# Dummy matmuls of 512 columns, a rectify moved to ScalarE and denominators a slot up, in the start of a cosFormer attention and mixture-of-experts kernel

## Chip, cores, metric

One NeuronCore of one Trainium2 chip. The metric is the device time of one execution in microseconds (us). Names used below: PE is TensorE (PEld its weight loads), DVE is VectorE, ACT is ScalarE, POOL is GpSimd, SP is SyncE.

## The reference

Linear (cosFormer) attention over 8 batches, whose output is the input of a dense mixture of 8 experts with Sinkhorn-balanced gates. Cut to what matters here:

```python
# attention: B, H, S, D = 8, 8, 576, 64
def phi(x, c, s):
    r = np.maximum(x, 0.0)                     # the "rectify"
    return np.concatenate([r * c, r * s], axis=-1)
q_p, k_p = phi(q, cos_w, sin_w), phi(k, cos_w, sin_w)
kv  = np.einsum('bhsf,bhsd->bhfd', k_p, v)
z   = np.sum(k_p, axis=2)
num = np.einsum('bhsf,bhfd->bhsd', q_p, kv)
den = np.einsum('bhsf,bhf->bhs', q_p, z)[..., None] + 1e-06
x   = num / den                                # then (4608, 512)
# gates: exp(x @ w_gate), 8 Sinkhorn rounds -> P
# for e in 8 experts: out += P[:, e] * (relu(x @ w1[e]) @ w2[e])
```

## The kernel before

The kernel is tuned already: PE works nearly all the time. Expert 0's matmuls for each batch (`ffn1`, `ffn2`) are woven in "slots" with the attention of the next batch. The parts that the change and the argument touch are these.

Dummy matmuls on a tile of ones keep PE busy while the first data is prepared (the first 80 run from 1.14 to 7.34 us), and are meant to keep its clock up. It is 1.00 in the trace from 4.4 to 21.5 us:

```python
def keep_busy(n):
    for _ in range(n):
        te.matmul(out=idle_ps[:, 0:P], lhsT=ones_sq[:], rhs=ones_sq[:], start=True, stop=True)
# [...] called with 80 at the start, 3 after each of 12 groups of turns, then 8, 5 and 18
```

k is rectified in place and multiplied by cos and sin. q likewise; the q of the first two batches is transposed by PE ("turns"), that of the later ones by DMA out of a pool of three `q_p` buffers:

```python
def prep_k(b, hk):
    k16 = loaded["k", b, hk]
    if b >= 2:
        se.activation(out=k16, in_=k16, func=AF.Relu)
    else:
        ve.tensor_scalar(out=k16, in0=k16, scalar1=0.0, scalar2=None, op0=ALU.max)

def prep_q(b, hk):
    # [...] (rectify on DVE if b >= 2)
    q_p = qp_pool.tile([P, C, 2, D], F16, name="q_p")          # qp_pool has bufs=3
    ve.tensor_tensor(out=q_p[:], in0=q16..., in1=cs, op=ALU.mult)
    if by_dma:                                                  # b >= 2
        qTs[b, hk] = q_pTs[(b * HK + hk) % len(q_pTs)]
        nc.sync.dma_start(out=qTs[b, hk], in_=q_p[:]..., transpose=True)
```

The inputs are loaded by POOL's queue, as early as buffers allow. The loads of the fourth batch (b = 3) are written at slot (1, 0), and in time run from 33 us on:

```python
            if j == 0:
                for half in range(2):
                    at(1, 0, load, b + 2, half)        # here b is 1: the fourth batch's q, k, v
            elif b + 2 < B:
                for half in range(2):
                    at(j, 11 + half, load, b + 2, half, "qkv", True)
```

`sums` makes k_p.T v, `denominators` multiplies z with qT and prepares the reciprocals `hl`, and `attend(b, hk)` reads `hl` (which makes its matmuls easy to find in the trace) and leaves the batch's part of x. As far as the traces were read, each engine runs its instructions in the written order: in that of the changed kernel a `k_p` of DVE stands behind a `q_p` that waits 1.91 us (shown below).

The softmax here doesn't subtract the row's maximum and nothing guards it: scores larger than these inputs give would overflow.

Of the kernel before, what the change touches and what calls it, by code (L numbers as in the profile page):

```python
# [25 lines left out]
def kernel(  # L26
# [11 lines left out]
    P = nc.NUM_PARTITIONS  # L38
# [12 lines left out]
    TCH = 512  # L51
# [129 lines left out]
    with ExitStack() as p1:  # L181
# [15 lines left out]
        def load(b, half, names="qkv", held_back=False):  # L197
# [24 lines left out]
        ones_sq = cs_pool.tile([P, P], F16, name="ones_sq")  # L222
# [3 lines left out]
            out=ident[:], in_=ones_sq[:], pattern=[[-1, P]], compare_op=ALU.is_equal,  # L226
# [15 lines left out]

        def keep_busy(n):


            for _ in range(n):
                te.matmul(
                    out=idle_ps[:, 0:P], lhsT=ones_sq[:], rhs=ones_sq[:], start=True, stop=True
                )

        idle_ps = ps_y.tile([P, Dm], FP32, name="y_ps")
        keep_busy(80)

        wrap = cs_pool.tile([P, C], FP32, name="wrap")
        ve.tensor_scalar(
            out=wrap[:], in0=gidx[:], scalar1=float(S), scalar2=None, op0=ALU.is_ge
# [3 lines left out]
            out=sval[:], in0=wrap[:], scalar=-float(S), in1=gidx[:],  # L260
# [9 lines left out]
        for hh in range(2):  # L270
            ve.tensor_copy(
                out=cs_half[hh * HP : (hh + 1) * HP, :, :, hh],
# [18 lines left out]
        with nc.allow_low_precision("sums of zeros and ones"):  # L291
            ve.tensor_reduce(
                out=lo[:], in_=rows[:, :, 1, :], axis=AX.XY, op=ALU.add, negate=True
# [3 lines left out]
                out=sel[:], in0=rows[:, 0:3, 0, :], in1=rows[:, 0:3, 1, :], op=ALU.add  # L297
            )
        ve.tensor_copy(
            out=spread.rearrange("p j hk hh d -> p (j hk hh) d"),  # L300
# [32 lines left out]

        def prep_k(b, hk):
            k16 = loaded["k", b, hk]
            if b >= 2:
                se.activation(out=k16, in_=k16, func=AF.Relu)
            else:
                ve.tensor_scalar(out=k16, in0=k16, scalar1=0.0, scalar2=None, op0=ALU.max)
# [27 lines left out]
        def prep_kp(b, hk):  # L367
            k16 = loaded.pop(("k", b, hk))
            k_p = kp_pool.tile([P, C, 2, D], F16, name="k_p")
            ve.tensor_tensor(  # L370
                out=k_p[:], in0=k16.unsqueeze(2).to_broadcast([P, C, 2, D]),
                in1=cs, op=ALU.mult,
            )
            kps[b, hk] = (
                k_p, v_augs[(b * HK + hk) % len(v_augs)] if b else loaded.pop(("v", b, hk))
            )
# [146 lines left out]
        def attend(b, hk):  # L523

            parts = ((0, 2 * C3), (2 * C3, C))
            rb_ps = [ps_s.tile([P, 512], FP32, name="small_ps") for _ in parts]
            rb = rb_pool.tile([P, C * HP], FP32, name="rb")
            for i, (c0, c1) in enumerate(parts):
                for j in range(c0 // C3, c1 // C3):
                    te.matmul(  # L530
                        out=rb_ps[i][:, (j * C3 - c0) * HP : ((j + 1) * C3 - c0) * HP],
                        lhsT=spread[0:96, j, hk].rearrange("p hh d -> p (hh d)"),
                        rhs=hls[b][:],
                        start=True,
                        stop=True,
                    )
                se.copy(out=rb[:, c0 * HP : c1 * HP], in_=rb_ps[i][:, 0 : (c1 - c0) * HP])
            num_ps = [ps_s.tile([P, 512], FP32, name="small_ps") for _ in parts]
            for i, (c0, c1) in enumerate(parts):
                for hh in range(2):  # L540
                    te.matmul(
                        out=num_ps[i][hh * HP : (hh + 1) * HP, 0 : (c1 - c0) * HP],
                        lhsT=kvs[b][0][:, hk, hh, :],
                        rhs=qTs[b, hk][:, c0:c1, hh * HP : (hh + 1) * HP],
                        start=True,
                        stop=True,
                    )
                ve.tensor_tensor(
                    out=xT[:, hk, b * S + c0 * HP : b * S + c1 * HP],
                    in0=num_ps[i][:, 0 : (c1 - c0) * HP],  # L550
                    in1=rb[:, c0 * HP : c1 * HP],
                    op=ALU.mult,
                )
# [25 lines left out]
        def at(block, slot, fn, *args):  # L579
            todo.setdefault((block, slot), []).append((fn, args))  # L580
# [19 lines left out]
        prep_kp(0, 1)  # L600
        denominators(0, range(0, 4))
        keep_busy(8)
        for hk in (2, 3):
            prep_k(0, hk)
# [16 lines left out]
        for hk in range(HK):  # L621
            attend(0, hk)
            for kt in ((), (0,), (1,), (2, 3))[hk]:
                for ft, h_ps in enumerate(first_ps):
                    te.matmul(
                        out=h_ps[:],
                        lhsT=w0[0][:, kt, ft * P : (ft + 1) * P],
                        rhs=xT[:, kt, 0:TCH],
                        start=(kt == 0),
                        stop=(kt == KT - 1),  # L630
                    )
                    if kt == KT - 1:
                        se.activation(out=hT[:, ft, 0:TCH], in_=h_ps[:], func=AF.Relu)
            for i in ((), (), (0,), (1, 2, 3))[hk]:
                prep_k(1, i)
                prep_kp(1, i)
        for hk in range(3):
            prep_q(1, hk)

        for j in range(B):  # L640
            b = j + 1
            if j == 0:

                def sums_first(half):
                    sums_made(1, half, sums_begun(1, half))

                for hk in range(HK):
                    for i in range(3):
                        at(0, (5, 6, 7, 7)[hk], turn, 1, hk, i, i != 1)
                    if hk == 0:  # L650
                        at(0, 5, prep_q, 1, 3)
                    if hk == 1:
                        at(0, 6, prep_v, 1, 0, se.copy)
                        at(0, 6, prep_v, 1, 2, ve.tensor_copy)
                    if hk == 2:
                        at(0, 7, prep_v, 1, 1, se.copy)
                        at(0, 7, prep_v, 1, 3, ve.tensor_copy)
                for half in range(2):
                    at(0, 7, sums_first, half)
                at(0, 9, denominators, 1)  # L660
                at(0, 10, gates, 0)
                for hk in range(HK):
                    at(0, 11 + hk, attend, 1, hk)
            elif b < B:
                if j == 1:
                    for hk in (2, 3):
                        at(j, 0, prep_q, b, hk)
                        at(j, 0, prep_k, b, hk)
                        at(j, hk - 2, prep_kp, b, hk)
                        at(j, hk - 2, prep_v, b, hk, se.copy)  # L670
                    at(j, 1, sums, b, 0)
                    at(j, 3, sums, b, 1)
                else:
                    at(j, 0, sums, b, 1)
                at(j, 5 if j == 1 else 3, denominators, b)
                for hk in range(HK):
                    at(j, (8 if j == 1 else 6) + 2 * hk, attend, b, hk)
            if j:
                at(j, 5, gates, j)
            if j == 0:  # L680
                for half in range(2):
                    at(j, 3, load, b + 1, half)
                for slot, fn, hk, *args in (
                    (12, prep_q, 0), (12, prep_k, 0), (13, prep_q, 1), (13, prep_k, 1),
                    (14, prep_kp, 0), (14, prep_v, 0, se.copy), (15, prep_kp, 1),
                    (15, prep_v, 1, se.copy),
                ):
                    at(j, slot, fn, b + 1, hk, *args)
            elif b + 1 < B:
                for slot, fn, hk in (  # L690
                    (3, prep_k, 0), (4, prep_q, 0), (4, prep_k, 1), (5, prep_q, 1),
                    (7, prep_kv, 0), (7, prep_k, 2), (7, prep_q, 2), (9, prep_q, 3),
                    (9, prep_k, 3), (9, prep_kv, 1), (11, prep_kv, 2), (13, prep_kv, 3),
                ):
                    at(j, slot + (j == 1), fn, b + 1, hk)
                at(j, 15 if j == 1 else 14, sums, b + 1, 0)
            if j == 0:
                for half in range(2):
                    at(1, 0, load, b + 2, half)
# [3 lines that stand above are left out]
# [490 lines left out]
    while stream:  # L1193
        _, pair, name = stream.pop(0)
# [32 lines left out]
```

## Time and profile before

| | before |
|---|---|
| time, median of 3 runs | 987.17 us (986.81 to 987.29) |
| span of the profiled run | 985.7 us |
| PE busy | 968.6 us (98%) |
| stop of PE with no releaser, at 17.5 us | 2.82 us |
| granted clock of 0.5 after it | 21.5 to 24.9 us |

From the page of the kernel before: the line of busy times (us, share of the span, number of instructions), and the shares of the chain that ended last.

```profile
PE 968.6 (98%) x7923; PEld 677.0 (69%) x7923; DVE 805.8 (82%) x1833; ACT 565.3 (57%) x1263; POOL 60.6 (6%) x82
...
PE 94%; DVE 2%; ACT 2%; issue 1%; POOL 0%; DMA 0%; ACTq 0%; SPq 0%; DVEq 0%; POOLq 0%
```

A kernel at 98% on its longest engine has only its start, its few waits and its end to give. The waits are read from the timeline of PE. Its columns are start and duration in us, engine, line, operation, output and inputs, shapes, count; in brackets the idle time of PE just before and what ended it. Of the kernel before:

```profile
16.66 0.79 PE L109 MATMUL y_ps<-ones_sq 128*128 128x128 f16 x11
20.27 0.55 PE L109 MATMUL y_ps<-ones_sq 128*128 128x128 f16 x7 [2.82 <-issue]
20.65 0.41 PE L109 MATMUL small_ps<-hl,acc_hi 96*128 96x192 f16 x3
...
31.95 0.68 PE L109 MATMUL small_ps<-ident,q_p 128*128 128x128 f16 x9 [0.76 <-DVE q_p L109]
...
44.01 0.42 PE L109 MATMUL small_ps<-hl,acc_hi 96*128 96x192 f16 x3 [0.35 <-DVE hl L109]
...
55.42 0.74 PE L109 MATMUL small_ps<-acc_lo,k_p 64*128 64x65 f16 x36
...
57.93 1.06 PE L109 MATMUL small_ps<-q_pT,zsel 128*32 128x192 f16 x24
...
62.02 0.41 PE L109 MATMUL small_ps<-hl,acc_hi 96*128 96x192 f16 x3
```

The stop of 2.82 us falls between the 11th and the 12th of 18 dummies, which wait for nothing. The lines that read `hl` at 20.65, 44.01 and 62.02 us are the first attends of the first, second and third batch: three milestones.

From the windows of the kernel before (window, its length, busy us and instructions of PE, PEld, DVE, ACT and POOL, then the granted TensorE clock, the DMA engines' share, GB/s):

```profile
18.00:20.00 2.00, 0.00 (x0) 0.00 (x0) 0.00 (x0) 0.00 (x0) 0.59 (x1) 1.00 1.28 196
20.00:22.00 2.00, 1.62 (x17) 1.06 (x16) 0.47 (x1) 0.70 (x2) 1.43 (x2) 0.88 1.42 198
22.00:25.00 3.00, 3.00 (x13) 1.19 (x11) 1.18 (x4) 0.70 (x2) 1.43 (x2) 0.51 1.23 208
```

After the stop the clock is at half for 3.41 us. The DMA engines are full all the while (share over 1).

### The profile page before, as it was taken

How to read it: one execution, taken by the hardware profiler on the slowest of the kernel's cores; microseconds unless marked ns; L12 is line 12 of the kernel's file. 1: busy time of each engine (PE TensorE's matmuls, PEld its weight loads, DVE VectorE, ACT ScalarE, POOL GpSimd, SP SyncE). 2: the span in 40 equal slices, each digit the busy share in tenths (PEclk: the TensorE clock that was granted, in tenths of full speed). 3: DMA queues.
4: the chain of work that ended last, by engine and by line, in shares of the span. 5: the costliest groups of instructions: out<-in, count | busy, mean ns of one | idle time of the engine just before them, and what ended most of it. 6: DMA issues, size and time to landing. Idle time of an engine off the chain costs nothing.

```text
span 985.7 us, 20379 instructions
## 1 busy us (share of the span) xinstructions
PE 968.6 (98%) x7923; PEld 677.0 (69%) x7923; DVE 805.8 (82%) x1833; ACT 565.3 (57%) x1263; POOL 60.6 (6%) x82
## 2 busy tenths in 40 slices
PE   8999999989999999999999999999999999999997
PEld 6444444447777777777777777777777777777775
DVE  5786774789889888988789888988888888987886
ACT  4676665467776555555555555555555555555551
POOL 6311110010000000000000000000000000000001
PEclk9999999999999999999999999999999999999999
DMA  9969990741013410133103400223103401104535
GB/s 164 206 120 161 156 152 10 136 76 48 34 41 67 88 29 26 50 67 67 50 25 68 91 25 25 60 60 66 49 25 75 85 25 35 39 25 119 130 88 123
DMA packets 80337, 73.56 MB, mean 75 GB/s; under 512 B 33264, under 2 KB 72176, under 8 KB 80240
## 3 DMA queue, kind: packets, MB, share of 16 engines
q0 software_dynamic: 27232, 30.94, 19.9%
q1 hardware_dynamic: 52768, 41.06, 16.9%
q8 instruction: 62, 1.02, 0.4%
q10 hardware_dynamic: 240, 0.26, 0.1%
q14 instruction: 35, 0.29, 0.1%
HBM read 83.12 MB, written 12.98 MB: 97 GB/s over the span
## 4 chain that ended last, share of the span: by engine, by line
PE 94%; DVE 2%; ACT 2%; issue 1%; POOL 0%; DMA 0%; ACTq 0%; SPq 0%; DVEq 0%; POOLq 0%
PE rows_ps L109 34%; PE h_ps L109 28%; PE copied_ps L109 11%; PE p_ps L109 11%; PE y_ps L109 6%; PE small_ps L109 4%; ACT acc_lo L109 0%; DVE k_p L109 0%; DVE acc_hi L900 0%; POOL hs_last L915 0%; DVE P_tok L109 0%; ACT hT L109 0%; DMA out_dram<-acc_lo 0%; DVE colp L109 0%; ACT u L109 0%
## 5 line engine op out<-in xcount | busy, mean ns | idle before, releaser
L900 DVE SCALAR_TENSOR_TENSOR acc_lo<-rows_ps,P_tok,acc_lo 128x512 f32<-128x512 f32 (+1 forms) x322 | 203.1, 639 | 74.8 <-PE rows_ps L109 74.6
L109 PEld LDWEIGHTS <-H 128*128 128x128 f16 x2080 | 203.0, 98 | 83.1 <-issue 1.2
L836 ACT CAST u<-h_ps 128x384 f16<-128x384 f32 x288 | 137.8, 478 | 131.1 <-PE h_ps L109 131.1
L109 PEld LDWEIGHTS <-w1e 128*128 128x128 f16 x1632 | 156.6, 98 | 67.5 <-issue 7.6
L830 DVE CUSTOM_DVE_ANT_0 H<-p_ps,u 128x384 f16<-128x384 f32 x329 | 180.8, 550 | 6.7 <-PE p_ps L109 6.6
L109 PEld LDWEIGHTS <-hs 128*128 128x128 f16 x1500 | 146.6, 98 | 56.2
L109 PE MATMUL h_ps<-S,w1e 128*128 128x384 f16 x672 | 164.1, 326 | 1.1 <-ACT u L109 0.9
L109 PE MATMUL p_ps<-xT,T 128*128 128x384 f16 x672 | 164.1, 326 | 0.1
L109 PE MATMUL h_ps<-xT,w1e 128*128 128x384 f16 (+1 forms) x616 | 150.5, 351 | 0.8 <-ACT hT L109 0.6
L109 PE MATMUL rows_ps<-V,H 128*128 128x256 f16 x1000 | 150.0, 273 | 0.7 <-DVE acc_hi L900 0.7
L109 PE MATMUL rows_ps<-w2e,hs 128*128 128x256 f16 x1000 | 150.0, 273 | 0.0
L868 ACT ACTIVATE H<-h_ps 128x384 f16<-128x384 f32 x144 | 70.7, 491 | 95.0 <-PE h_ps L109 95.0
L109 PEld LDWEIGHTS <-T 128*128 128x128 f16 x1008 | 98.1, 98 | 29.2 <-issue 2.8
L109 PE MATMUL rows_ps<-w2e,H 128*128 128x256 f16 (+1 forms) x568 | 91.2, 285 | 0.0
L849 ACT COPY copied_ps<-h_ps 128x384 f32<-128x384 f32 x144 | 67.5, 468 | 35.2 <-PE h_ps L109 35.2
L859 ACT ACTIVATE H<-copied_ps 128x384 f16<-128x384 f32 x144 | 70.9, 492 | 20.3 <-PE copied_ps L109 20.3
L109 PE MATMUL h_ps<-S,T 128*128 128x384 f16 x336 | 81.8, 325 | 0.3 <-ACT copied_ps L109 0.3
L109 PE MATMUL copied_ps<-xT,w1e 128*128 128x384 f16 x336 | 82.1, 326 | 0.0
L109 PE MATMUL copied_ps<-w2e,H 128*128 128x256 f16 x504 | 75.5, 272 | 0.0
L109 PE MATMUL rows_ps<-V,hs 128*128 128x256 f16 x500 | 75.0, 272 | 0.0
L900 DVE SCALAR_TENSOR_TENSOR acc_lo<-copied_ps,P_tok,acc_lo 128x256 f32<-128x256 f32 x126 | 60.0, 476 | 0.5
L900 DVE SCALAR_TENSOR_TENSOR acc_hi<-rows_ps,P_tok,acc_hi 128x512 f32<-128x512 f32 (+1 forms) x56 | 41.2, 736 | 20.5 <-PE rows_ps L109 19.7
(147 smaller groups left out, 953.2 us busy)
## 6 DMA issues: line engine op xcount, KB each, us to landing
S<-x_saved SPq DMA_DIRECT2D x108, 192.0 KB, 2.4
out_dram<-acc_lo SPq DMA_DIRECT2D x62, 128.0 KB, 2.4
w1e<-in_moe_w_dram POOLq DMA_DIRECT2D x7, 1024.0 KB, 8.9
w2e<-in_moe_w_dram POOLq DMA_DIRECT2D x7, 1024.0 KB, 9.6
q_ld<-in_q_dram POOLq DMA_DIRECT2D x16, 288.0 KB, 7.5
k_ld<-in_k_dram POOLq DMA_DIRECT2D x16, 288.0 KB, 8.3
v_ld<-in_v_dram POOLq DMA_DIRECT2D x16, 288.0 KB, 9.6
x_saved<-S SPq DMA_DIRECT2D x18, 192.0 KB, 1.9
```

The costliest lines, as they stand in the source:

```text
L109: i = getattr(self.engine, name)(*args, **kwargs)
L830: latest = ve._custom_dve(TENSOR_ADD_SAT, out=out, in0=ps[:, 0:TU], in1=t[:], s0=FP32_MAX, s1=0.0)
L836: se.copy(out=t[:], in_=ps[:, 0:TU])
L849: se.copy(out=Y[:, 0:TU], in_=X[:, 0:TU])
L859: se.activation(out=h11, in_=Y[:, 0:TU], func=AF.Relu)
L868: se.activation(out=h12, in_=X[:, 0:TU], func=AF.Relu)
L900: ve.scalar_tensor_tensor(out=a, in0=rows, scalar=P_tok[:, g, self.e : self.e + 1], in1=a, op0=ALU.mult, op1=ALU.add,)
```

## The change

Its intent: fewer PE instructions for the same dummy time (so that instructions are fetched in time), less work for DVE in front of the second batch's q, and the denominators early enough for DVE's reciprocal chain to be hidden.

```diff
         def keep_busy(n):
-            for _ in range(n):
+            for cols in [TCH] * (n // 4) + [n % 4 * P] * (n % 4 > 0):
                 te.matmul(
-                    out=idle_ps[:, 0:P], lhsT=ones_sq[:], rhs=ones_sq[:], start=True, stop=True
+                    out=idle_ps[:, 0:cols],
+                    lhsT=ones_sq[:],
+                    rhs=ones_sq[:, 0:1].to_broadcast([P, cols]),
+                    start=True,
+                    stop=True,
                 )
@@ prep_k
-            if b >= 2:
+            if b:
                 se.activation(out=k16, in_=k16, func=AF.Relu)
@@ after attend(0, hk) and its share of ffn1
-            for i in ((), (), (0,), (1, 2, 3))[hk]:
+            for i in ((), (0,), (1, 2), (3,))[hk]:
                 prep_k(1, i)
+            for i in ((), (0,), (1,), (2, 3))[hk]:
                 prep_kp(1, i)
@@ slots of the first block
-                at(0, 9, denominators, 1)
+                at(0, 8, denominators, 1)
```

## The prediction

> **What bounds the kernel now.** TensorE is 968.6 of 985.7 us busy (98%, the page); the chain that ended last is 94% PE. From 60 us on, 10 us windows show PE busy throughout, but for about 4 us in the Sinkhorn part. The change touches only the first 60 us: what it saves moves the end one for one, but is a few us.
>
> The timeline of PE shows three losses there:
> 1. PE stops from 17.45 to 20.27 us, 2.82 us, amid the 18 dummies, releaser "issue". I read it as an instruction fetch: the instruction queue moved a packet from 17.78 to 18.72. [...] packets of 16 KiB, 256 PE instructions apart (boundaries at the 189th, 445th, 701st). While loads fill the DMA engines, each starts about 3.7 us after PE crosses a boundary (8.24 to 11.82, 14.07 to 17.78, 20.27 to 23.97) and serves some 2.5 us later: 6.2 us for 256 instructions, which dummies of 56 ns and 64-row matmuls of 16 ns (two instructions each) outrun.
> 2. After that stop the granted clock is 0.5 from 21.5 to 24.9 us; matmuls of 512 columns stand 0.42 us apart instead of 0.22: some 1.4 us.
> 3. DVE's k rectify and k_p hold q_p: PE idles 0.76 us at 31.2; later 0.35 us at 43.7, for hl.
>
> **What changes.** Dummies: the same columns and time, 212 PE instructions fewer. The boundaries shift: the 189th instruction is now in the first key sums (about 11.4 us), the 445th in the second half of the kv sums (16.3 us), the 701st past the turns, where PE is slow. The fetch triggered at 11.4 should serve about 17.5. So the stop does not vanish: I expect 1.2 us (0.5 to 2) there, and the first attend at 18.9 instead of 20.65: 1.7 us. A stop of 1.2 us should not drop the clock (1.1 us idle around 31 us did not): 1.4 us more.
>
> ScalarE takes four k rectifies: DVE loses 4 x 0.30 us, ACT gains 4 x 0.6 us. Three fall among the rb copies and delay the last of these by some 0.3 us. The fourth is queued behind four hT activations; k_p(3) and q_p wait for it: PE's idle before the first turns grows from 0.76 to about 1.5 us. Net cost 0.5 us.
>
> The denominators a slot up put three y_ps blocks (0.9 us each) behind them instead of two; DVE's den chain (2.5 us) is then covered: 0.35 us.
>
> **Sum.** 1.7 + 1.4 - 0.5 + 0.35 = 2.9 us. Predicted 984.3 us, range 982.2 to 986.3. Faster by over 2%: 0.01; within 2%: 0.98; slower: 0.01.
>
> **Right if** the profile shows: the "issue" stop near 16 to 17.5 us, about 1.2 us long; no clock of 0.5 near 21 to 25; the fourth k rectify after hT; PE's idle before the first turns longer, that before the second batch's attend gone; from 60 us on the same events 3 us earlier.
>
> **Wrong if** the fetch comes sooner (no stop: 1.3 us better) or later, or the stop still halves the clock (1.4 us worse); if the fourth rectify costs PE more, or the longer idle at 27 to 29 us halves the clock; if loads, whose landing doesn't move, become the limit; or if a shifted boundary makes a new stop before 45 us.

The "boundaries" are every 256th PE instruction, matmuls and weight loads counted: the pages show 62 packets of 16 KB on the instruction queue q8 for 15846 of them before the change, and 61 for 15634 after it, one per 256.

## More of the kernel before

The lines at 55.42 (sums) and 57.93 (denominators) of the third batch run without a wait.

From the list of DMA issues of the kernel before, 44 to 60 us: the transposes of the third batch's q, their number and the median us from issue to landing.

```profile
q_pT<-q_p SPq DMA_TRANSPOSE x4, 3.5
```

## The result, and the profile after

Ratios are the mean time of one kernel's fast runs over that of the other's fast runs of the same rounds, so they are not quite the ratio of the medians quoted beside them.

| | before | after |
|---|---|---|
| time, median of 4 runs each | 986.99 us (986.72 to 987.29) | 986.49 us (986.31 to 987.08) |
| ratio, 95% interval | | 0.9996 (0.9979 to 1.0013) |
| span of the profiled run | 985.7 us | 985.4 us |
| first attend of batch 1, 2, 3 | 20.65, 44.01, 62.02 us | 19.23, 41.69, 62.63 us |

The forecast was 984.3 us, at most 986.3. The measured 986.49 us lies outside: nearly nothing was gained. The profiled run was the slowest of the four, but the others gained no more than 0.7 us against the median before.

From the page of the changed kernel:

```profile
PE 967.8 (98%) x7817; PEld 671.3 (68%) x7817; DVE 805.8 (82%) x1829; ACT 566.7 (58%) x1267; POOL 60.6 (6%) x82
...
PE 94%; DVE 2%; ACT 2%; DMA 1%; issue 0%; POOL 0%; SPq 0%; ACTq 0%; DVEq 0%; POOLq 0%
```

106 matmuls and as many weight loads fewer, as meant. In the chain that ended last "issue" gave its 1% to "DMA". These shares are rounded, so the line is only a hint: a wait for instructions may have been traded for a wait for transfers. The timeline of PE of the changed kernel, the same places as before:

```profile
16.00 0.88 PE L109 MATMUL small_ps<-v_ld,k_p 64*128 64x64 f16 x48
17.78 0.53 PE L109 MATMUL small_ps<-v_ld,k_p 64*128 64x64 f16 x24 [0.91 <-issue]
...
19.23 0.41 PE L109 MATMUL small_ps<-hl,acc_hi 96*128 96x192 f16 x3
...
30.15 0.68 PE L109 MATMUL small_ps<-ident,q_p 128*128 128x128 f16 x9 [1.61 <-DVE q_p L109]
...
41.69 0.41 PE L109 MATMUL small_ps<-hl,acc_hi 96*128 96x192 f16 x3
...
53.09 0.46 PE L109 MATMUL small_ps<-acc_lo,k_p 64*128 64x65 f16 x18
55.26 0.46 PE L109 MATMUL small_ps<-acc_lo,k_p 64*128 64x65 f16 x18 [1.70 <-DVE k_p L109]
...
57.48 0.68 PE L109 MATMUL small_ps<-q_pT,zsel 128*32 128x192 f16 x18
59.25 0.35 PE L109 MATMUL small_ps<-q_pT,zsel 128*32 128x192 f16 x6 [1.10 <-DMA q_pT<-q_p]
...
62.63 0.41 PE L109 MATMUL small_ps<-hl,acc_hi 96*128 96x192 f16 x3
```

Up to 41.69 us all goes as foreseen, and PE is 2.32 us ahead. Then come two waits that the kernel before does not have, 1.70 and 1.10 us, and at the third milestone PE is 0.61 us behind. From there on the two traces run in step: at PE's last instruction the changed kernel is 0.76 us behind (981.05 against 980.29 us), and only the tail of the last stores differs in its favour. The windows of the changed kernel show the full clock where it was at half:

```profile
20.00:22.00 2.00, 1.75 (x13) 0.94 (x12) 1.64 (x5) 1.58 (x5) 0.79 (x2) 1.00 1.44 204
22.00:25.00 3.00, 3.00 (x23) 1.36 (x21) 2.51 (x6) 2.44 (x6) 1.43 (x2) 1.00 1.22 203
```

What does `k_p` wait for at 53 us? The timeline of DVE of the changed kernel:

```profile
51.56 0.30 DVE L109 TENSOR_SCALAR q_ld<-q_ld 128x576 f16<-128x576 f16 x1
53.77 0.76 DVE L109 TENSOR_TENSOR q_p<-q_ld,acc_hi 128x1152 f16<-128x1152 f16 x1 [1.91 <-DMA q_pT<-q_p]
54.45 0.75 DVE L109 TENSOR_TENSOR k_p<-k_ld,acc_hi 128x1152 f16<-128x1152 f16 x1
```

The fourth `q_p` of the third batch goes into the first of three buffers, and so waits for the transpose that reads it; `k_p`, which PE needs, stands behind it in DVE's order. And the transposes are late. The DMA issues of the changed kernel from 44 to 60 us, and its DMA queues from 46 to 49 us (packets, MB, share of 16 engines):

```profile
q_pT<-q_p SPq DMA_TRANSPOSE x4, 5.4
```

```profile
q0 software_dynamic: 570, 0.62, 121.0%
```

They take 5.4 us at the median instead of 3.5. The first was issued at 46.09 us, and in the 3 us from 46 to 49 not one packet of the transposes' queue (q1) moved: q0, the loads from POOL, had all of the DMA engines. In the trace its packets start at 49.11 us, 3.0 us after the issue; in the kernel before the first was issued at 48.41 us and its packets start at 49.75, 1.3 us after. In both the stream of loads dies down near 49 to 51 us. It does so at the same time because the loads had filled the DMA engines almost since the start (their share is 1.02 or more in every window read from 4 to 49 us, in both kernels); PE's lead did not shorten it: from 49 to 50 us q0 still starts 157 packets before the change and 151 after it, from 50 to 51 us 55 and 61.

The second wait, 1.10 us, is of another kind. The last packet of the loads starts at 52.37 us, before the third and fourth transposes are issued (52.69 and 54.62 us). The DMA queues of the changed kernel from 56 to 59 us:

```profile
q1 hardware_dynamic: 1050, 0.26, 103.5%
q8 instruction: 1, 0.02, 2.4%
```

No load moves here. Beside the transposes there is one packet of 16 KB of q8, the instruction queue whose packets go with PE's count (one per 256 of its instructions, above), from 56.57 to 57.71 us. From 57 us on the transposes' packets stall (20 took over 1 us), and the fourth transpose lands at 59.21 us, 4.6 us after its issue (3.5 us in the kernel before). There PE's wait ends. (A landing is here the last of the transfer's 16 records in the trace.) So the traces point to the loads for the first wait, and beside the second they show an instruction fetch that fell into a transpose. The runs below test the first; none was made to test the second by itself.

### The profile page after: what moved, and what is told of

Read it like the earlier page. It is cut to its first block, busy times and chain, and to the rows that moved or that the text cites. A ratio compares the mean times of both kernels' runs of the same rounds, so it can differ in the third digit from the quotient of the medians.

```text
span 985.4 us, 20168 instructions
## 1 busy us (share of the span) xinstructions
PE 967.8 (98%) x7817; PEld 671.3 (68%) x7817; DVE 805.8 (82%) x1829; ACT 566.7 (58%) x1267; POOL 60.6 (6%) x82
## 4 chain that ended last, share of the span: by engine, by line
PE 94%; DVE 2%; ACT 2%; DMA 1%; issue 0%; POOL 0%; SPq 0%; ACTq 0%; DVEq 0%; POOLq 0%
PE rows_ps L109 34%; PE h_ps L109 27%; PE copied_ps L109 11%; PE p_ps L109 11%; PE y_ps L109 6%; PE small_ps L109 4%; DMA q_pT<-q_p 1%; ACT hT L109 0%; DVE acc_hi L904 0%; POOL hs_last L919 0%; DVE P_tok L109 0%; DMA out_dram<-acc_lo 0%; DVE colp L109 0%; ACT u L109 0%; ACT acc_lo L109 0%
```

## The experiments

**Theory A**: PE's lead is taken back because the third batch's q transposes now come before the end of the stream of loads (whose last are the fourth batch's v) and wait for it. **Theory B**: the rectify on ACT loses the lead, by way of the changed order. Two further questions are whether the stop at 17 us is an instruction fetch, and what the fourth rectify costs. Each kernel ran 5 timed rounds (6 for one) on the same chip as the others of its group; the kernel before on those chips had medians of 987.5, 986.58 and 987.09 us.

The milestones of all profiled runs (first attend of the second and third batch, read from the timeline of PE; then when the third batch's first transpose was issued, and when it landed) tell most of the story:

| kernel | 2nd batch, us | 3rd batch, us | between | transpose issued | landed |
|---|---|---|---|---|---|
| before | 44.01 | 62.02 | 18.01 | 48.41 | 52.55 |
| after | 41.69 | 62.63 | 20.94 | 46.09 | 53.68 |
| dummies_only | 42.06 | 62.28 | 20.22 | 46.47 | 53.05 |
| rectify_only | 43.60 | 61.40 | 17.80 | 48.01 | 52.97 |
| denoms_only | 44.99 | 62.77 | 17.78 | 49.38 | 53.19 |
| moved | 40.21 | 62.30 | 22.09 | 44.61 | 53.19 |
| hold_v | 41.95 | 62.18 | 20.23 | 46.35 | 50.43 |
| before_longer | 42.46 | 66.45 | 23.99 | 46.87 | 56.20 |
| before_hold_v2 | 42.98 | 60.78 | 17.80 | 47.38 | 50.78 |
| hold_v2 | 40.79 | 58.58 | 17.79 | 45.19 | 50.27 |
| hold_v2_moved | 40.24 | 58.03 | 17.79 | 44.64 | 50.02 |
| hold_v2_dve4 | 39.42 | 60.24 | 20.82 | 43.82 | 51.01 |
| best2 | 38.12 | 59.40 | 21.28 | 42.53 | 50.12 |
| best3 | 38.91 | 57.01 | 18.10 | 43.31 | 47.36 |

Undisturbed, the stretch takes 17.8 us. With the loads as they were (the first six rows), the third batch's attend comes between 61.4 and 62.8 us, whether the second's came at 40.2 or at 45.0. Coming early can even end later: rectify_only reached the second at 43.60 us and the third at 61.40, moved at 40.21 and 62.30.

The last two columns show why. With the loads as they were, the first transpose landed between 52.55 and 53.68 us, whether it was issued at 44.61 or at 49.38 us. With the fourth batch's v held back it landed between 50.02 and 51.01 us, with more held back at 47.36, and with two more loads at 56.20. For all that are issued early, the loads and not the issue set when it lands.

### dummies_only: the dummies alone

The kernel before with the new `keep_busy` and nothing else of the change.

> The kernel before with the dummy part of the change alone. Theory A (the lead won by 45 us is taken back because the third batch's q transposes by DMA run into the fourth batch's loads, which fill the DMA engines until about 51 us whatever PE does): the 2.8 us stop shrinks to about 1.1 us, no clock of 0.5, PE 3 us or more ahead of before at 45 us, then new waits between 50 and 60 us (k_p or q_p, and the denominators for q_pT) of 2.5 to 4 us; time 986.0 to 987.0. Theory B (the rectify on ScalarE is what loses the lead): no such waits, and 983.3 to 984.3.

Measured: 986.53 us against 987.5 (ratio 0.9994, 0.9981 to 1.0007), within A's range and 2 us above B's. From its timeline of PE:

```profile
18.32 0.53 PE L109 MATMUL small_ps<-v_ld,k_p 64*128 64x64 f16 x24 [1.21 <-issue]
...
54.62 0.46 PE L109 MATMUL small_ps<-acc_lo,k_p 64*128 64x65 f16 x18 [0.69 <-DVE k_p L109]
...
58.90 0.35 PE L109 MATMUL small_ps<-q_pT,zsel 128*32 128x192 f16 x6 [1.38 <-DMA q_pT<-q_p]
```

Both new waits are there without any rectify on ACT, 2.07 us together. Here, too, the loads had ended (last packet at 51.5 us) before the second one, and an instruction packet for PE ran from 56.80 to 57.68 us. Of the fourth transpose's 16 landing records, 15 are there by 57.29 us, before PE begins to wait at 57.52; the last comes at 58.86, where the wait ends. The lead at the second milestone was 1.95 us, less than the 3 us that I had expected, since in this run PE's first turns came 1.1 us later than in the profile of before (8.86 us against 7.78). Theory B cannot explain the waits.

### rectify_only: the rectify alone

The kernel before with the two edits of `prep_k` and its place.

> The kernel before with the k rectify on ScalarE alone. Both theories: the 2.8 us stop and the 0.5 clock stay; PE's idle before the first turns grows from 0.8 to about 1.6 us. Theory A: PE comes later, so the transposes meet less of the loads; 987.0 to 987.9. Theory B: new waits between 50 and 60 us appear here too, 988.5 or more.

Measured: 987.03 us against 987.5 (ratio 0.9998, 0.9985 to 1.0011). From its timeline of PE:

```profile
31.56 0.62 PE L109 MATMUL small_ps<-ident,q_p 128*128 128x128 f16 x8 [1.61 <-DVE q_p L109]
...
43.60 0.42 PE L109 MATMUL small_ps<-hl,acc_hi 96*128 96x192 f16 x3 [0.35 <-DVE hl L109]
...
61.40 0.41 PE L109 MATMUL small_ps<-hl,acc_hi 96*128 96x192 f16 x3
```

The idle time before the turns is 1.61 us, as in the changed kernel, and no wait follows between 50 and 60 us. Theory B falls. Its stop was 2.33 us, but this time the clock did not fall. My "both theories: the 0.5 clock stays" was wrong: the clock's fall is not a fixed consequence of the stop (see the last section).

### denoms_only: the denominators alone

The one line `at(0, 8, denominators, 1)`.

> The kernel before with the denominators a slot up alone. Both theories: the 0.35 us wait for hl before the second batch's first attend goes. It is so small a lead that the loads should not take it back wholly: 986.5 to 987.1, span 0 to 0.4 us shorter.

Measured: 986.88 us against 987.5 (ratio 0.9994, 0.9981 to 1.0008). The wait for `hl` is gone, and from the first turns to the second batch's attend PE takes 11.55 us (33.44 to 44.99) instead of 12.06 (31.95 to 44.01): 0.5 us. The total cannot show it, since this profiled run had 6.83 us of half clock after its stop.

### hold_v: the fourth batch's v loads later

The changed kernel with a shorter stream of loads:

```diff
                 for half in range(2):
-                    at(1, 0, load, b + 2, half)
+                    at(1, 0, load, b + 2, half, "qk")
+                    at(1, 1, load, b + 2, half, "v", True)
```

> The changed kernel, but the fourth batch's v loads are held back to the next slot (after the third batch's q_p work), so that the other loads end about 3 us sooner. Theory A: the transposes land sooner, the 1.7 us wait for k_p and the 1.1 us wait for q_pT shrink to under 1 us together, time 984.0 to 985.3. Theory B, or transposes that are slow for another reason than the loads: waits stay, 986 to 987.

Measured: 987.22 us against 987.5 (ratio 0.9998, 0.9985 to 1.001): a miss for A as I had put it. From its timeline of PE:

```profile
58.80 0.35 PE L109 MATMUL small_ps<-q_pT,zsel 128*32 128x192 f16 x6 [2.26 <-DMA q_pT<-q_p]
```

The wait for k_p is gone, the wait for q_pT doubled. In the trace the first pair of transposes is through by 51.0 us, as hoped, but the held loads start to move at 55.75 us, while the second pair is at its end: its last 32 of 2368 packets come only between 56.8 and 58.0 us. The collision had been moved, not removed. (An instruction packet for PE, 57.76 to 58.64 us, falls near the end of it; its share is not separated.)

### hold_v2: later still

The changed kernel again, v held back to the last matmul of the third batch's denominators, when all four transposes have landed. It computes the same.

```diff
-                    at(1, 0, load, b + 2, half)
+                    at(1, 0, load, b + 2, half, "qk")
@@ block 1, after its denominators
                 at(j, 5 if j == 1 else 3, denominators, b)
+                if j == 1:
+                    for half in range(2):
+                        at(1, 5, load, b + 1, half, "v", te)
@@ load: held back to DVE's last instruction (True) or to the given engine's
-                    after(ve.last, i)
+                    after((ve if held_back is True else held_back).last, i)
```

> The changed kernel, with the fourth batch's v loads held back until the third batch's denominators (their last matmul), so that neither pair of the third batch's transposes shares the DMA engines with them. In hold_v the first pair was freed (no wait for k_p), but the held loads started at 55.8 us and met the last packets of the second pair (2.3 us wait for q_pT). Theory A (collision of transposes and loads): both waits are gone or under 0.5 us together, PE keeps its lead of 2 us or more from 52 us on; median 983.2 to 984.6. If the transposes are slow for another reason: a wait for q_pT of over 1 us stays and 986 to 987.3.

Measured: 983.66 us (982.79 to 984.14) against 986.58: ratio 0.9967 (0.9955 to 0.998). As A said. From its timeline of PE, and its DMA queues from 46 to 49 us:

```profile
52.20 0.75 PE L109 MATMUL small_ps<-acc_lo,k_p 64*128 64x65 f16 x36
...
54.70 0.84 PE L109 MATMUL small_ps<-q_pT,zsel 128*32 128x192 f16 x24
...
58.58 0.41 PE L109 MATMUL small_ps<-hl,acc_hi 96*128 96x192 f16 x3
```

```profile
q1 hardware_dynamic: 674, 0.17, 75.7%
q0 software_dynamic: 240, 0.25, 49.2%
```

Sums (36 in one line) and denominators (24 in one line) run without a wait again, and the lead is kept. For the second wait this is no test of the loads: the fourth transpose, issued at 51.84 us, landed at 55.12, and an instruction packet (54.56 to 55.48 us) came only at its end. In the same window of time in which the changed kernel's transposes moved no packet, they now move 674.

### before_hold_v2: the control

> The same holding back in the kernel before, as a control. Theory A: there the first transposes are issued at 48.4 us and start 1.3 us later without waiting, so taking loads away gives nothing: 986.3 to 987.6, no more than 0.5 us from before. If holding back v is worth something by itself: 984 to 985.5.

The same edit on the kernel before: 986.63 us against 986.58 (ratio 0.9999, 0.9987 to 1.0012). Shorter loads by themselves give nothing: without the change PE never reaches them early enough. The gain needs both.

### before_longer: the cost, brought on on purpose

The kernel before with two more loads of the same size, into a scratch tensor in HBM that nobody reads; the result stays right.

```diff
                 for half in range(2):
                     at(1, 0, load, b + 2, half)
+                at(1, 0, more_loads)   # two DMAs, each like one load of q, to scratch tensors
```

> The kernel before with two more loads of the same size (to a scratch tensor in HBM), so that the stream of loads ends about 2.8 us later, while PE comes as before. Theory A: the first transposes start at 51.5 us or later instead of 49.8, PE waits for k_p or q_pT 1 to 3 us between 53 and 60 us; median 988 to 990. If transposes don't suffer from loads: 986.5 to 987.5.

Measured: 991.33 us against 986.58 (ratio 1.0038, 1.0024 to 1.0052), over my range. From its timeline of PE, and its window of 57 to 60 us:

```profile
57.78 0.68 PE L109 MATMUL small_ps<-acc_lo,k_p 64*128 64x65 f16 x18 [3.45 <-DVE k_p L109]
```

```profile
57.00:60.00 3.00, 2.22 (x22) 1.09 (x23) 1.37 (x6) 0.43 (x2) 0.00 (x0) 0.51 0.74 148
```

The same wait as in the changed kernel appears in the kernel before, and is longer. What I had left out is that the clock could fall with the wait: in this run, with a wait of 3.45 us, it is at half for 6.83 us from 57.05 us on. Two things differ from what I had expected. The first transpose's packets started at 50.80 us, not at 51.5 or later, and then ran slowly beside the loads. And PE did not come "as before": in this profiled run the clock had not fallen after the first stop, so it was 1.55 us early (42.46 against 44.01 us at the second batch), and a part of the wait is that lead.

### moved: is the stop an instruction fetch?

The changed kernel, with 64 of the first dummies narrow again and 4 wide: 96 PE instructions more for the same columns. It shifts every boundary of 256 PE instructions (one q8 packet per 256 in the pages of before and after) and nothing else.

```diff
-        keep_busy(80)
+        for _ in range(64):
+            te.matmul(out=idle_ps[:, 0:P], lhsT=ones_sq[:], rhs=ones_sq[:], start=True, stop=True)
+        keep_busy(16)
```

> The changed kernel with 64 of the first dummies of 128 columns again and 4 of 512: 96 PE instructions more, the same columns and time. It moves the boundaries of 256 PE instructions: the 189th instruction comes in the second group of turns (about 9 us instead of 12), the 445th in the second half of the denominators (about 15.5 us). Fetch theory: served about 15.3 us, so the stop of 1.1 us shrinks to under 0.3 us, and the first attend comes 0.7 to 1.1 us sooner than in the changed kernel. By theory A the transposes take that back: 985.8 to 987. If the stop is not a fetch: it stays at about 1.1 us in the kv sums.

Measured: 986.72 us against 986.58 (ratio 0.9998, 0.9986 to 1.0011). From its timeline of PE:

```profile
15.44 1.22 PE L109 MATMUL small_ps<-v_ld,k_p 64*128 64x64 f16 x72
16.60 1.15 PE L109 MATMUL y_ps<-ones_sq 128*128 128x512 f16 x5
17.73 0.42 PE L109 MATMUL small_ps<-hl,acc_hi 96*128 96x192 f16 x3
...
54.77 0.46 PE L109 MATMUL small_ps<-acc_lo,k_p 64*128 64x65 f16 x18 [2.70 <-DVE k_p L109]
```

The stop is gone: 72 matmuls in one line instead of 48, a stop and 24. More instructions, placed better, cost less than fewer. This is what the fetch theory expected (under 0.3 us; otherwise 1.1 us), and so confirms the fetch. (How much the stop costs is better read from hold_v2 and hold_v2_moved below, whose first turns came at the same time, 7.77 and 7.79 us: 0.55 us at the first and at the second batch's attend. The changed kernel's first turns came 0.6 us later than those of moved.) And the 1.5 us of lead over the changed kernel are taken back by a longer wait, 2.70 us, after which the clock is at half from 56.1 to 59.6 us.

### hold_v2_moved, hold_v2_dve4, best2, best3: how far it goes

`hold_v2_moved` is hold_v2 with the first dummies of moved. `hold_v2_dve4` is hold_v2 with `if b and (b, hk) != (1, 3)` in `prep_k`, so the fourth rectify is back on DVE. `best2` has both. `best3` is best2 with the second halves of the fourth batch's k and q held back to the same matmul as v.

> hold_v2 with the page boundary moved as in moved. Fetch theory and theory A together: no stop in the sums, PE 1.0 us earlier than in hold_v2 until the transposes; these are issued at about 44.2 us, while the held-back stream of loads still ends at about 48 us, so that part of the 1.0 us may be taken back. Between hold_v2 minus 1.0 and hold_v2: median 982.5 to 983.9.

> hold_v2 with the second batch's fourth k rectify back on VectorE, before its k products. PE's idle before the first turns falls from about 1.6 to 0.8 us; the transposes are issued 0.8 us sooner and meet more of the loads. If what the fourth rectify costs on ScalarE is real and not hidden: 0.3 to 0.8 us below hold_v2, median 982.7 to 983.7; if hidden by the transposes: the same as hold_v2.

> hold_v2 with both: boundary moved, fourth rectify on VectorE. PE is 1.8 us earlier than in hold_v2 at 40 us; theory A says that the transposes, issued at about 43.4 us, still start only near 47 us, so that waits for k_p or q_pT of 1 us or more come back: median 982.2 to 983.7, less than 1.8 us below hold_v2.

> best2 with the second halves of the fourth batch's k and q held back too, behind the same matmul. The stream of loads ends at about 45 us, so the third batch's transposes start within 2 us of their issue and the waits of best2 go; but the held loads (5.6 us of DMA from about 56 us) now meet the fourth batch's first transposes and are needed from 60 us on. Theory A: 981.3 to 983 if the work of the fourth batch has slack, up to 985 with new waits from 60 to 72 us if not.

| kernel | this, us | ratio to before, 95% interval | waits of PE, 50 to 70 us |
|---|---|---|---|
| hold_v2_moved | 983.47 | 0.9959 (0.9947 to 0.9971) | none new |
| hold_v2_dve4 | 983.73 | 0.996 (0.9947 to 0.9973) | k_p 1.30, q_pT 1.38 |
| best2 | 983.3 | 0.9959 (0.9948 to 0.9971) | k_p 1.71 |
| best3 | 986.11 | 0.9987 (0.9975 to 0.9999) | xT 3.52 |

(The kernel before: 987.09 us in the same rounds.) The fourth rectify is worth a good deal where it stands: in the timeline of DVE of hold_v2, `k_p` waits

```profile
27.76 0.76 DVE L109 TENSOR_TENSOR k_p<-k_ld,acc_hi 128x1152 f16<-128x1152 f16 x1 [2.46 <-ACT k_ld L109]
```

and with that one rectify on DVE, PE needs 9.15 us from its first attend to the second batch's turns (18.74 to 27.89) instead of 10.92 (18.32 to 29.24). But with 1.4 us more of lead (39.42 against 40.79 us at the second batch's attend) the transposes come into the loads again: they are issued at 43.82 instead of 45.19 us, while the stream of loads ends near 48 to 49 us. The lead is taken back: 1.30 us by the wait for k_p, and 1.38 us by one for q_pT, beside which the trace again has an instruction packet (54.74 to 55.70 us) in the fourth transpose, long after the loads. Holding back more (best3, a miss: I had expected 985 at most) frees the transposes, which then start 1.3 us after their issue, but the held k, q and v arrive too late for the fourth batch: DVE waits 3.8 us for v, PE 3.5 us, and the clock falls for 6.83 us. So all three good versions end between 983.3 and 983.7 us, and their ranges overlap; none can be called the best. Each beats the kernel before in the same rounds (intervals below 1). The changed kernel was not timed beside them, but its fastest run (986.31 us) is slower than the slowest of theirs (984.66). A fourth `q_p` buffer, which would spare DVE the wait for the first transpose, was not tried.

## Why the prediction was wrong, point by point

- **The stop**: right. Predicted 1.2 us (0.5 to 2) in the second half of the kv sums; measured 0.91 us in the bracket, ending at 17.78 us (predicted 17.5). `moved` confirms that it is a fetch. In the traces, counting matmuls and their weight loads, the stop always comes after PE's 700th instruction with the old dummies (5 profiles) and after its 444th with the new (5 profiles), 256 apart, as the q8 packets are on average (255.6 instructions each before, 256.3 after).
- **The clock**: right for the changed kernel, whose four runs had a mean granted clock of 0.999 to 1.0. But the 1.4 us were not a fixed cost of the kernel before: its timed runs in the three groups had 0.996 to 0.999 and took 985.6 to 988.9 us. All 14 runs of after, dummies_only and hold_v2 had 0.999 to 1.0, so with the new dummies the fall at the start is at least rarer. But the predicted 1.4 us measured the profile of before, not the kernel before. (The idle time around 31 us that the prediction leans on is a single stop of 0.76 us in the trace, not 1.1; the 1.61 us there in the changed kernel did not drop the clock either.)
- **First attend**: predicted 18.9, measured 19.23 us, with the first turns 0.76 us later than in the profile of before (8.54 against 7.78).
- **The rectify on ACT**: right. The idle time before the turns was 1.61 us (predicted 1.5). Its net cost was predicted as 0.5 us; from first attend to the turns, rectify_only takes 10.93 us (20.63 to 31.56) against 10.31 of before_hold_v2 (20.61 to 30.92), the same stretch with neither the rectify moved nor a low clock: 0.6 us.
- **The denominators**: predicted 0.35, measured 0.5 us.
- **The sum up to 41.69 us**: 2.32 us ahead of the profile of before, and 3.22 in hold_v2 (40.79 us), whose first turns came as early as there (7.77 us); predicted 2.9. Against before_hold_v2, where the clock did not fall (42.98 us), the two are only 1.29 and 2.19 us ahead: that the sum fits is in part luck of the draw.
- **The step that failed** is in the first paragraph and in the last line of "Right if": "what it saves moves the end one for one" and "from 60 us on the same events 3 us earlier". The runs showed in its place that PE, between 50 and 60 us, depends on transposes by DMA, which in the changed kernel got no packet through from 46.09 to 49.11 us, when the stream of loads ebbed. That kernel issued the first of them 2.3 us sooner (46.09 against 48.41 us), but it landed 1.1 us later (53.68 against 52.55), and PE waited 1.70 us for k_p. The other 1.10 us, for q_pT, came after the loads, when an instruction packet for PE fell into the fourth transpose. The same stands in the traces of dummies_only and hold_v2_dve4, 1.38 us each; no run tests it alone. The prediction had looked for the effect of shifted boundaries only up to 45 us. The prediction named loads as a possible limit under "Wrong if", but took PE's waits in the profile of before as all there could be, and so neither sized it nor let its range hold it.

It could have been seen before: the transposes were issued at 48.41 us in the kernel before, their packets started 1.3 us later, and the loads ended at 51.0 us. They stood at the edge of the stream already, with no slack to give.

What stays open is why a transpose gets no packet for up to 3.9 us under the loads (moved and before_longer), and whether and why one instruction packet holds up a transpose. That the first goes away with the loads is shown (from 46 to 49 us 674 packets of the transposes in hold_v2, none in the changed kernel); what brings it about is not.

## What to carry to other kernels

Before a gain at the start is carried through to the end, look for the next event whose time is set by something that the change does not move, such as the end of a stream of transfers, and measure how far before it the dependent work now arrives: the gain is capped there, and coming early may even cost, however busy the compute engine looks after it. A waiting time of zero in the profile says nothing of how much earlier one could come. Then move the cap with the change: here, loads that were not needed yet were held back, which gave nothing alone, and with the change gave about 3 us (983.66 against 986.58).

## What else the traces showed

- Transposes beside loads: in the changed kernel the transposes' queue moved no packet from 46 to 49 us, with the first issued at 46.09 and the loads' queue at 121% of the engines; its packets started 3.0 us after the issue, and 1.3 us after it where the loads were already dying down (before, hold_v2). Whether they stood ready in that time no trace shows; in before_longer both queues did move packets together, from 50.80 us on.
- The cost of a fetch: while the loads filled the DMA engines (share 1.03 or more in the windows read from 4 to 30 us of before), a fetch's packet started 3.6 to 3.7 us after PE crossed a boundary (its 95th, 223rd and 351st matmul, at 8.24, 14.07 and 20.27 us of before; the packets at 11.82, 17.78 and 23.97). PE, stopped for 2.82 us, went on 2.5 us after the start of the second of them; in the changed kernel, stopped for 0.91 us, it went on 2.5 us after a packet that had started at 15.26 us, 3.1 us after its 95th matmul. In both the packet that follows one crossing came before the stop at the next, 256 instructions on, ended.
- The clock after a stop: it fell to half after stops of PE of 2.82 us (before, then 3.41 us at half), 2.2 us (denoms_only, 6.83 us) and 1.71 us (best2, 3.41 us); stops of 2.33 us (rectify_only) and 2.26 us (hold_v) did not bring it down. So the length of the stop alone does not decide it; what does, no run here shows.
- An instruction fetch beside another queue's transfer: in dummies_only, 15 of the fourth transpose's 16 landing records came by 57.29 us and the last at 58.86, with one instruction packet of 16 KB from 56.80 to 57.68 us and no loads; PE waited 1.38 us. This is read from traces (after and hold_v2_dve4 show the like), not tested.
